# Eighty-eight tiny products on a tile of zeros at the head of TensorE's program

## The chip, the cores and the metric

The kernel runs on one core of a Trainium2 chip. The metric is the device time of one execution in microseconds; before the change its median over 3 runs is 282.65 us (282.52 to 283.0). All stage times below are counted from the first instruction of the one profiled execution.

## What is computed

Eight batches of eight heads of linear attention, and a feed-forward layer on its output:

```python
q_s = softmax of q over its last axis (64)          # q, k, v: (8, 8, 576, 64), float32
k_s = softmax of k over the sequence (576)
kv  = einsum('bhsd,bhse->bhde', k_s, v)
x   = einsum('bhsd,bhde->bhse', q_s, kv)            # as 4608 tokens x 512
h   = x @ w_in                                      # 512 -> 2048
g   = h + sin(alpha * h)**2 / (alpha + 1e-09)
out = g @ w_out                                     # 2048 -> 512
```

## The kernel before

The work is cut in two ways. Attention goes by batch: q, k and v of a batch are loaded as [128, 4, 9, 64] tiles (two heads side by side over the partitions), ScalarE takes the exponentials (`exp_half`, `exp_to`, L117), `kv_mm` (L172) sums k and v over the sequence in 36 small products per half batch, `kv_norm` (L182, L183) divides, and `attn_x` (L216) multiplies the transposed, normalised q (`q_transpose_ii`, L199) by the result. The output goes into `xT`, bf16, with the model dimension on the partitions. The feed-forward part goes by tiles of 512 tokens, nine in all: `mm_h` (L261) makes one of 16 blocks of h from `win` in four accumulating products with the inner index k in the order 0, 2, 1, 3; `sine` (L267, L269 or L271 or L273) and `combine` (L277) make g; `mm_o` (L281) multiplies g by `wout`.

The order on each engine is the order of the program text: nothing is moved by a scheduler. The text is written by hand so that batch 0 is brought through attention first, in halves named `ii`, and then its 512 tokens go through `mm_h` while batch 1 is loaded and worked on.

The head, which the change touches, runs like this:

- SP issues the loads of batch 0 (L306): q half 0, k half 0, q half 1, v half 0, k half 1, then alpha (L311).
- GpSimd builds an identity, VectorE copies it to bf16 (`identb`, L313) and sets `zero` and the ones columns of `vb` (L315, L317). GpSimd then copies one element of the first k half (`held`, L334), which holds it back until that half has landed, and only then issues v half 1 (two DMAs, L306), eight DMAs of `win` (L107: first columns 0 to 511 of k blocks 0 and 2 in two pieces, then of blocks 1 and 3 in one piece of 512 KB, then the rest) and two of `wout` (L110). These convert from float32 to bf16 on the way.
- TensorE starts with seven products of the identity with the first exponentials, 128 weight columns by 512 moving columns each, into a PSUM tile `warm` that nobody reads (`warm_up(7)`, L349). Then come eight transposes of q half 0 (L199), two more such products, `kv_mm` for half 0, one more such product, a small transpose of alpha (L384), eight transposes of q half 1, `attn_x`, `kv_mm` for half 1, the k = 0 and k = 1 products of the first blocks of h, `attn_x` for half 1, and the loop over 16 blocks of h. In the first four blocks the loop adds the last two k.
- In that loop, `late` gives SP the loads of batch 1: q half 0 behind block 6, q half 1 and then k and v in halves (L452) behind block 12, each behind a VectorE write of one element into the buffer (L443).

Behind that loop stands the product with `wout` for the first token tile, interleaved with the attention of batch 1; its two `kv_mm` calls need the casts of v (`cast_v1`, L470, ScalarE and GpSimd), and each cast needs its half of v.

Of the kernel before, what the change touches and what calls it, by code (L numbers as in the profile page):

```python
# [16 lines left out]
BF16 = mybir.dt.bfloat16  # L17
# [6 lines left out]
def kernel(  # L24
# [14 lines left out]
    nc = tc.nc  # L39
# [15 lines left out]
    singles = ctx.enter_context(tc.tile_pool(name="singles", bufs=1))  # L55
# [249 lines left out]
    def load0(eng, n, t, ii, j0=0, j1=J):  # L305
        eng.dma_start(out=staged[n, 0][:, ii::2, j0:j1].rearrange("p i j d -> p i (j d)"),  # L306
                      in_=src_view(t, 0)[:, ii::2, j0 * D:j1 * D])

    for n, t, ii in (("q", q, 0), ("k", k, 0), ("q", q, 1), ("v", v, 0), ("k", k, 1)):
        load0(nc.sync, n, t, ii, 0, 8 if n == "q" else J)  # L310
    nc.sync.dma_start(out=alpha_rows, in_=moe_alpha.rearrange("(no ni) -> no ni", ni=128))  # L311
    make_identity(nc, ident)
    DVE_CP(identb, ident)  # L313
    zero = singles.tile([128, 1], F32, name="zero")
# [8 lines left out]

    tp0 = ps_h[0].tile([128, 8, 128], BF16, name="tp", tag="a")
    warm = ps_h[0].tile([128, 4, 128], F32, name="warm", tag="a")

# [380 lines left out]
```

## Time and profile before

| | us |
|---|---|
| median of 3 runs (range) | 282.65 (282.52 to 283.0) |
| the profiled execution's own time | 282.79 |
| its span, first to last instruction | 281.0 |
| outside the span | 1.8 |
| TensorE busy in the span | 267.7 (95%) |
| ScalarE, VectorE, GpSimd busy | 223.8, 185.5, 81.3 |
| HBM traffic, mean over the span | 164 GB/s |

The profile's busy time of TensorE is an upper view, since matmuls are pipelined and overlap in it: a product of 512 moving columns shows as 379 ns, while in a dense stretch the next one starts 216 ns later (eight of them span 1.73 us in the chain of waits). A line of the timeline gives the start, the length, the engine, the line, the operation with its output and inputs, the count, and in brackets the idle time of the engine ahead of it and what ended that. The views used are the chain that ended last, the timeline, the waits, the busy time by windows and the DMA queues. The trace also holds one record for each DMA packet; the sixteen 4-byte packets with which a load signals its end (one for each DMA engine) show when each of the sixteen engines finished its part.

### The profile page before, as it was taken

What the parts mean: (1) busy time and instruction counts of PE and PEld (TensorE: products, weight loads), DVE (VectorE), ACT (ScalarE), POOL (GpSimd) and SP (SyncE); (2) the same over time, 40 slices, a digit from 0 to 9 for tenths busy, and PEclk for the clock granted to TensorE, in tenths of its full rate; (3) what the DMA queues carried; (4) which work ended last, traced back from release to release, by engine and by line L of the source; (5) the groups of instructions that cost most, each with busy time, mean ns of one, the idle gap of its engine ahead of it and who ended that gap; (6) DMA issues with size and microseconds to landing.
All of it is one profiled execution on the core that took longest, in us unless ns stands there. A gap on an engine that the chain in (4) does not pass through costs nothing.

```text
span 281.0 us, 4925 instructions
## 1 busy us (share of the span) xinstructions
PE 267.7 (95%) x1890; PEld 124.0 (44%) x1919; DVE 185.5 (66%) x279; ACT 223.8 (80%) x322; POOL 81.3 (29%) x77
## 2 busy tenths in 40 slices
PE   2899989999999999999999999999999999999994
PEld 1444444444443444444444444444444444444443
DVE  3968776899878767766776677577775555555412
ACT  5899458999588999899989998999877777777400
POOL 2968121777667460205003500350000000000000
PEclk9999999999999999999999999999999999999999
DMA  7999999997599039712991199125011111111143
GB/s 263 299 194 232 278 307 319 361 343 253 120 229 399 2 81 334 290 37 48 267 383 45 37 263 392 38 50 124 8 29 40 37 37 37 40 41 42 40 106 75
DMA packets 39320, 45.82 MB, mean 163 GB/s; under 512 B 17008, under 2 KB 22656, under 8 KB 39296
## 3 DMA queue, kind: packets, MB, share of 16 engines
q1 hardware_dynamic: 33392, 40.58, 46.9%
q0 software_dynamic: 5744, 4.79, 10.3%
q8 instruction: 15, 0.25, 0.3%
q10 hardware_dynamic: 160, 0.13, 0.2%
q14 instruction: 9, 0.07, 0.1%
HBM read 36.71 MB, written 9.44 MB: 164 GB/s over the span
## 4 chain that ended last, share of the span: by engine, by line
PE 85%; DMA 8%; POOL 2%; issue 1%; SPq 1%; ACT 1%; DVE 1%; ACTq 0%
PE op L281 38%; PE hp L261 38%; DMA st_v<-in_v_dram 4%; DMA win<-in_moe_w_in_dram 2%; PE lp L261 2%; PE kvp L172 2%; DMA st_k<-in_k_dram 2%; PE op L261 1%; PE op L679 1%; POOL s L271 1%; PE kvp L261 1%; PE hp L216 1%; PE xp L216 1%; POOL st_v L306 1%; DVE g L277 1%
## 5 line engine op out<-in xcount | busy, mean ns | idle before, releaser
L277 DVE SCALAR_TENSOR_TENSOR g<-s,inva_sb,hp 128x512 bf16<-128x512 f32 x128 | 94.5, 746 | 58.7 <-ACT s L269 53.3
L261 PE MATMUL hp<-xT,win 128*128 128x512 bf16 x506 | 127.7, 379 | 0.6 <-PE lp L216 0.2
L281 PE MATMUL op<-wout,g 128*128 128x512 bf16 x478 | 121.0, 379 | 1.6 <-issue 1.1
L267 ACT ACTIVATE s<-hp,alpha_sb 128x512 f32<-128x512 f32 x128 | 86.1, 682 | 22.3 <-PE hp L261 21.0
L261 PEld LDWEIGHTS <-win 128*128 128x128 bf16 x576 | 55.7, 98 | 67.8 <-DMA win<-in_moe_w_in_dram 1.2
L281 PEld LDWEIGHTS <-g 128*128 128x128 bf16 x560 | 53.4, 98 | 64.8 <-issue 2.3
L269 ACT ACTIVATE s<-s 128x512 f32<-128x512 f32 x112 | 70.5, 630 | 3.5
L271 POOL TENSOR_TENSOR s<-s 128x512 f32<-128x512 f32 x29 | 30.1, 1053 | 17.6 <-ACT s L267 11.3
L151 POOL TENSOR_TENSOR qn<-qe,qs 128x1152 bf16<-128x1152 bf16 x11 | 23.2, 2127 | 29.5 <-DVE qs L145 24.4
L293 DVE COPY o<-op 128x512 f32<-128x512 f32 (+2 forms) x33 | 21.8, 661 | 10.2 <-PE op L281 7.9
L136 POOL CAST vb<-st_v 128x1152 bf16<-128x1152 f32 x12 | 14.7, 1257 | 45.6 <-DMA st_v<-in_v_dram 45.6
L117 ACT ACTIVATE qe<-st_q 128x1152 bf16<-128x1152 f32 (+2 forms) x18 | 17.7, 1025 | 6.1 <-DMA st_q<-in_q_dram 6.0
L117 ACT ACTIVATE ke<-st_k 128x1152 bf16<-128x1152 f32 x16 | 17.9, 1151 | 3.2 <-DMA st_k<-in_k_dram 3.2
L144 DVE TENSOR_REDUCE qs<-qe 128x36 f32<-128x2304 bf16 x5 | 12.8, 2551 | 8.3 <-ACT qe L117 8.3
L117 ACT ACT_TABLE_LOAD x7 | 9.0, 1283 | 0.8 <-PEq L693 0.7
L172 PE MATMUL kvp<-vb,ke 64*64 64x65 bf16 x576 | 6.9, 194 | 2.2 <-ACT vb L470 1.5
L349 PE MATMUL warm<-qe,identb 128*128 128x512 bf16 x10 | 4.1, 554 | 5.0 <-ACT qe L117 5.0
L281 PE MATMUL hp<-wout,g 128*128 128x512 bf16 x31 | 8.6, 379 | 0.1
L172 PEld LDWEIGHTS <-ke 64*64 64x64 bf16 x576 | 6.0, 106 | 6.1 <-issue 3.4
L281 PE MATMUL lp<-wout,g 128*128 128x512 bf16 x30 | 8.4, 379 | 0.2 <-issue 0.2
L261 PE MATMUL lp<-xT,win 128*128 128x512 bf16 x30 | 7.5, 379 | 0.1
L229 DVE CAST xT<-xp 128x1024 bf16<-128x1024 f32 (+1 forms) x7 | 7.4, 1065 | 0.0
(89 smaller groups left out, 135.8 us busy)
## 6 DMA issues: line engine op xcount, KB each, us to landing
out_dram<-o SPq DMA_DIRECT2D x70, 128.0 KB, 2.4
st_q<-in_q_dram SPq DMA_DIRECT2D x6, 1152.0 KB, 6.3
st_k<-in_k_dram SPq DMA_DIRECT2D x6, 1152.0 KB, 8.6
st_v<-in_v_dram SPq DMA_DIRECT2D x6, 1152.0 KB, 11.3
st_k<-in_k_dram SPq DMA_DIRECT2D x4, 576.0 KB, 8.1
st_q<-in_q_dram SPq DMA_DIRECT2D x4, 512.0 KB, 6.0
st_v<-in_v_dram SPq DMA_DIRECT2D x3, 576.0 KB, 10.0
wout<-in_moe_w_out_dram POOLq DMA_DIRECT2D x3, 512.0 KB, 12.7
```

What stands on the lines that cost most here:

```text
L117: nc.scalar.activation(dst[:, :, ii * 128:(ii + 1) * 128].rearrange("p j (x d) -> p x j d", x=2), src[:, ii::2], AX.Exp)
L136: engs[ii](vv[:, 2 * ii:2 * ii + 2, :, 0:D], staged["v", b][:, ii::2])
L144: nc.vector.tensor_reduce(qs, A["qe", b].rearrange("p j (i d) -> p j i d", i=4), axis=AXL.X, op=ALU.add)
L151: engs[ii % len(engs)].tensor_tensor(qn[:, ii, 0:j1].rearrange("p j (x d) -> p j x d", x=2), qe[:, ii], part.unsqueeze(3).to_broadcast([12 ...
L172: nc.tensor.matmul(kvp[64 * x:64 * x + 64, e, ii * 65:(ii + 1) * 65], ke[r, j, h * 64:(h + 1) * 64], vt[r, j, h * 65:(h + 1) * 65], start= ...
L261: nc.tensor.matmul(hp, win[:, KO[k], ni * 128:(ni + 1) * 128], xT[:, KO[k], t * MF % NX:t * MF % NX + MF], start=(k == 0), stop=(k == 3))
L267: nc.scalar.activation(s, hp, AX.Sin, scale=alpha_sb[:, ni:ni + 1])
L269: nc.scalar.activation(s, s, AX.Square)
L271: nc.gpsimd.tensor_tensor(s, s, s, op=ALU.mult)
L277: nc.vector.scalar_tensor_tensor(G[t][:, ni], in0=s, scalar=inva_sb[:, ni:ni + 1], in1=hp, op0=ALU.mult, op1=ALU.add)
L281: nc.tensor.matmul(acc, G[t][:, ni, j * 128:(j + 1) * 128], wout[:, ni, :], start=(ni == 0), stop=(ni == nN - 1))
L293: eng(o[:, cols], acc)
```

## The change

A bf16 tile of zeros, `tiny`, is made by VectorE ahead of the copy of the identity. At the head of TensorE's program, ahead of the seven products of `warm_up(7)`, stand 88 products of 64 columns of that tile, as weights, with one moving column of it. They take partitions 0 to 63 and 64 to 127 in turn, write the same half of the partitions of `warm`, one column, and nobody reads the result.

```diff
     nc.sync.dma_start(out=alpha_rows, in_=moe_alpha.rearrange("(no ni) -> no ni", ni=128))
+    tiny = singles.tile([128, 64], BF16, name="tiny")
+    nc.vector.memset(tiny, 0.0)
     make_identity(nc, ident)
     DVE_CP(identb, ident)
...
     warm = ps_h[0].tile([128, 4, 128], F32, name="warm", tag="a")
+    for n in range(88):
+        r = slice(64 * (n % 2), 64 * (n % 2) + 64)
+        nc.tensor.matmul(warm[r, 0, 0:1], tiny[r], tiny[r, 0:1], start=True, stop=True)
```

Each product is two instructions, a weight load and a matmul, so TensorE's program grows from 3839 to 4015 rows, 176 more. VectorE has one instruction more. The order of everything else, on every engine and queue, is as before. All line numbers behind L313 grow by 2 and those behind L325 by 5.

## The prediction

> **What bounds the kernel now.** I read the chain that ended last first, from its start, because the change sits at the head. Each line is start, length, engine and line.
>
> ```profile
> 1.26 4.42 DMA st_k<-in_k_dram
> 5.92 1.56 POOL st_v L306 x2
> 7.48 1.43 POOL win L107 x2
> 8.90 5.92 DMA win<-in_moe_w_in_dram
> 14.87 1.90 PE hp L261 x8
> ...
> 29.41 12.43 DMA st_v<-in_v_dram
> 41.86 0.75 ACT vb L470
> ```
>
> The reader is to see that TensorE is not in the chain for the first 14.87 us. It runs from the k load (landed 5.68) through GpSimd's DMA issues to the 512 KB piece of `win` (landed 14.83). From 14.87 the dense TensorE stream carries it; then the second v half of batch 1, issued at 29.41 and landed at 41.84, sets the end of the stretch. Behind that TensorE alone carries it (85% of the chain).
>
> The timeline of the head, by engine, shows what TensorE does meanwhile.
>
> ```profile
> 4.98 3.15 PE L349 MATMUL warm<-qe,identb 128*128 128x512 bf16 x7 [4.98 <-ACT qe L117]
> ...
> 7.84 0.77 PEld L199 LDWEIGHTS <-qn 128*128 128x128 bf16 x8 [0.62 <-DVE qn L364]
> 7.92 0.87 PE L199 MATMUL tp<-identb,qn 128*128 128x128 bf16 x8
> 8.50 1.17 ACT L331 CAST vb<-st_v 128x1152 bf16<-128x1152 f32 x1 [0.33 <-DMA st_v<-in_v_dram]
> ...
> 9.57 1.00 ACT L378 COPY qT<-tp 128x1024 bf16<-128x1024 bf16 x1
> ...
> 9.72 0.48 PE L172 MATMUL kvp<-vb,ke 64*64 64x65 bf16 x36 [0.50 <-ACT vb L331]
> ...
> 10.61 0.62 PE L199 MATMUL tp<-identb,qn 128*128 128x128 bf16 x8
> ...
> 14.87 3.14 PEld L261 LDWEIGHTS <-win 128*128 128x128 bf16 x16 [0.57 <-DMA win<-in_moe_w_in_dram]
> ```
>
> Two things. The eight transposes take 0.87 at 7.92 and 0.62 at 10.61; the seven warm-up products go at 427 ns start to start (5.79, 6.22, 6.64, 7.07 in the weight loads' lines) where the dense stream goes at 216. So TensorE is at half speed until about 8.5 us and at full speed after. (The granted clock reads 1.00 in the windows from 0 on, so the half-speed stretch is seen only in durations.) And every step of this stretch waits for something else: the transposes for VectorE's `qn` (7.80), `kv_mm` for ScalarE's cast (9.66), which waited for v's DMA; the stream at 14.87 for `win`.
>
> **The change, part by part.**
>
> *The memset.* One short VectorE instruction (the two memsets of 36 columns took 0.09 each) ahead of the identity copy, which waits for GpSimd until 1.34 while VectorE is idle. Nothing.
>
> *The 88 products on TensorE.* The trace has no such shape. Below: `kv_mm`'s 36 products of 64 weight columns and 65 moving ones took 0.41 us in the windows view (9.72 to 10.13), 11.4 ns each at full speed with four quarters of the array in turn; 88 of them 1.0 us. Above: the half-speed transposes, 107 ns each (seven steps from 7.92 to about 8.6), 9.4 us. I take the nearer row, `kv_mm`, times two for half speed and two for using two quarters, not four: 46 ns, 4.0 us. Starting near 0.9 (VectorE is free at 0.75) they end near 4.9, when the first exponentials release the warm-up (4.98). TensorE was idle there, so they cost nothing. An end 1 us later is still hidden: warm-ups at full speed take 1.5 us instead of 3.0, and the first hard date is the transposes at 7.84. At the upper bound they would end at 10.3, and the head would slip by some 2.5 us; I give that 3%.
>
> *What an earlier full clock saves.* Warm-ups 1.5 us, transposes 0.4, ending near 8.4 instead of 8.8. Their reader, ScalarE's copy, starts at 9.57 because ScalarE is in the cast until 9.67. So what is late next is the same cast, and the saving on the path is 0. From 8.6 on TensorE is at full speed in both. If the products don't raise the clock, the cost is also 0.
>
> [...]
>
> *176 more instructions to fetch.* This is the part that touches the path. The page's queue list:
>
> ```profile
> q8 instruction: 15, 0.25, 0.3%
> ```
>
> Fifteen packets of 16.4 KB (0.25 MB over 15) against 3809 recorded TensorE instructions on the page: one packet for 254 instructions, so this is TensorE's code. By the trace's packet records they start at 15.93, 37.62, 49.25 and so on and take 0.9 to 1.3 us each on one DMA engine. They are requested ahead of need: by the fourth (67.91) 1042 instructions had already started. I expect no code stall. But each holds up the engine that carries it. By the 4-byte end packets, from the 15.93 packet on one engine finishes each load later than the other fifteen: 20.65 against 19.87, 23.19 against 22.42, and, with the second packet at 37.62, the last v half at 41.45 against 40.03. That late engine is what landed v at 41.84.
>
> With 176 instructions ahead, packets come 176 instructions earlier. The first was asked for at some 244 started instructions; 244 - 176 = 68 lies in `kv_mm` (rows 35 to 107, at 9.72). With the same delay of about 1.06 us (14.87 to 15.93) it starts near 10.8. The 512 KB piece of `win` lies then on that engine. Its end packets lie at 13.68 to 14.52; the late engine loses about 1.1 (20.65 against a typical 19.5). If it was among the first twelve (13.68 to 14.06) it ends at 14.8 to 15.2, and the dense stream starts 0.3 to 0.7 later: **+0.45** there. The second packet moves to instruction 454 - 176 = 278, at about 20 us, and may hold the last piece of `win`, wanted at 23.5, by up to 0.9; together up to about **+1.0** at block 12.
>
> What hides it: `kv_mm` idles 0.22 and 1.24 us (waits view, L172 on vb) for v, which lands by that DMA engine's load, not by TensorE. Before 41.45 that engine carried two code packets; now two as well, if the third comes after its last v packet. The third falls at instruction 524 to 531, in `kv_mm` of batch 1 (39.18 to 39.6, or 0.8 later since its v half is then the one delayed), plus 1.06: 40.4 to 41.5, on the edge. A hit costs one packet: 0.5 to 0.95. The later issue of the loads (27.87 to 29.41, behind the stream) can pass on between 0 and its 0.45; DMA ran at 200 to 290 GB/s until 33 and 400 after, so part is made up; I take 0.2.
>
> [...]
>
> *Sum.* 0 (memset) + 0 (products, under the idle 4.98) + 0 (clock, under the cast) + 0.2 = +0.2 us. The profiled execution's 282.79 (281.0 of span and 1.8 outside) gives 283.0; it stands 0.14 above the median, so from the median 282.65 I say **282.9**.
>
> **The rivals.** 0.2%, 0.57 us, is about what a measurement of this kernel can tell from no change.
>
> 1. *No measurable change*, the forecast: 282.1 to 283.2. For: TensorE is off the chain until 14.87 and idle 1.46 us before 42.65. Against: the landing at 41.84 hangs on one engine. 47%.
> 2. *Slower: the third code packet, or the delayed stream, reaches the v landing.* Place: the load of 29.41 to 41.84. Price: 0.5 to 0.95 for the packet, up to 0.45 for the issue; 0.6 to 1.2 together, 283.3 to 283.9. It decides if the packet starts ahead of that engine's last v packet (41.45). For: my estimate straddles it. Against: a v half that comes late delays the request. 34%. With the 3% of products far too slow (285): 37%.
> 3. *Faster: the second code packet leaves the v load.* It sat at 37.62, inside that load. If the engine makes up the earlier packet before 36 (rates fall to 200 GB/s at 29 to 31) and the third misses, v lands 0.9 earlier and the 1.24 us wait shrinks: 281.8 to 282.0. 16%.
> 4. *The products don't raise the clock* (the trace shows no such product, so it can't tell). Same time as 1 or 2, told by the warm-up products' pace; part of those cases.
>
> **Chances and range.** Same 0.47, slower 0.37, faster 0.16. The likeliest case's own range is 282.1 to 283.2; taking in both prices, 281.9 to 284.0.
>
> **What would show it.** The warm-ups at 4.98 starting 216 ns apart, not 427, and the transposes at 7.8 taking about 0.62: the clock step. Those transposes still waiting for `qn` near 7.8 and `kv_mm` for the cast near 9.7: no gain in the head. The first code packet near 10.8 and `win` landing at 15.1 to 15.5: the fetch step. The wait of `kv_mm` near 42.65 shorter than 1.24 with v landing near 41.8: absorbed; landing near 42.5: rival 2; near 41: rival 3. I am wrong if the products run past 7.8, if TensorE's clock falls again in the idle stretch that faster warm-ups leave before 7.8, or if the gap at 14.87 moves for another reason.

## The result and the profile after

The changed kernel takes 284.84 us (median of 14 runs, 283.83 to 286.83), the kernel before 282.88 in the same rounds (14 runs, 281.88 to 285.4): a ratio of 1.0074, 95% interval 1.0056 to 1.0093, or +2.1 us. The forecast of 282.9 and its range up to 284.0 were too low. The profiled execution took 284.82 us with a span of 283.0; before it was 282.79 and 281.0.

The timeline of the head of the changed kernel (start, length, engine, line, operation, idle time ahead of it):

```profile
0.96 2.50 PE L330 MATMUL warm<-tiny 64*64 64x1 bf16 x88 [0.96 <-DVE tiny L313]
...
5.29 3.15 PE L354 MATMUL warm<-qe,identb 128*128 128x512 bf16 x7 [1.83 <-ACT qe L117]
...
8.23 0.99 PE L199 MATMUL tp<-identb,qn 128*128 128x128 bf16 x8
...
10.23 1.17 ACT L336 CAST vb<-st_v 128x1152 bf16<-128x1152 f32 x1 [1.61 <-DMA st_v<-in_v_dram]
11.30 1.00 ACT L383 COPY qT<-tp 128x1024 bf16<-128x1024 bf16 x1
11.45 0.48 PE L172 MATMUL kvp<-vb,ke 64*64 64x65 bf16 x36 [1.80 <-ACT vb L336]
...
12.34 1.00 PE L199 MATMUL tp<-identb,qn 128*128 128x128 bf16 x8
...
16.27 3.78 PEld L261 LDWEIGHTS <-win 128*128 128x128 bf16 x19 [0.23 <-issue]
```

Three things differ from before. The products end at about 3.4 and don't change the clock: the warm-up products still take 3.15 us, and the first transposes 0.99. ScalarE's cast of v half 0, at 8.50 before, starts at 10.23, behind an idle 1.61 us that a DMA ended; TensorE waits 1.80 for it. And the second set of transposes, 0.62 before, takes 1.00: TensorE is at half speed again. The busy time by windows shows that directly, in the column PEclk (third from the right; the others are length, busy time and count of the five engines, and after the clock the DMA share and GB/s):

```profile
9.00:12.00 3.00, 1.20 (x42) 0.71 (x40) 1.91 (x4) 1.77 (x2) 3.00 (x5) 1.00 1.12 332
12.50:15.50 3.00, 2.82 (x51) 1.77 (x49) 2.31 (x6) 2.00 (x4) 2.57 (x4) 0.50 1.36 200
16.00:19.00 3.00, 3.00 (x17) 1.33 (x18) 0.69 (x1) 2.59 (x5) 0.00 (x0) 1.00 1.45 196
```

The second difference, the late cast, starts where the v load was in flight. The DMA queues of the changed kernel between 6.5 and 7.5 us:

```profile
q1 hardware_dynamic: 187, 0.39, 102.9%
...
q8 instruction: 1, 0.02, 6.5%
```

The first packet of TensorE's code starts at 6.89 us by its record (15.93 before), with 187 instructions started, in the middle of SP's loads. Of the sixteen end packets of v half 0, fifteen come between 7.93 and 8.41; the sixteenth not before 9.40; the load has landed at 10.21, and the cast follows at 10.23. Before, all sixteen came between 7.79 and 8.11, and the load had landed at 8.48.

Instruction by instruction, VectorE and ScalarE run the same sequence in both kernels (VectorE but for the memset), so their delays can be followed. They are +0.3 at the first exponentials (4.61 for 4.30; in e9 below, which has no products in the head, the first q load lands as late), +1.73 at the cast and +2.73 where the dense stream starts. Then the waits for v of batch 1 take back part: +1.0 at ScalarE's second cast of v (42.89), +1.1 on VectorE from 44.3 us on. Then it grows again, on ScalarE to +2.0 at 47 us, and stays there to the end. The late part is a wait of ScalarE for the small load of the last q columns (`q8`). First before, then after, from the timeline of ScalarE:

```profile
45.13 0.74 ACT L117 ACTIVATE qe<-q 128x256 bf16<-128x256 f32 x2
```

```profile
47.13 0.72 ACT L117 ACTIVATE qe<-q 128x256 bf16<-128x256 f32 x2 [0.90 <-DMA q<-in_q_dram]
```

TensorE pays for it at the transposes of q8. The waits of TensorE from 44 us on in the changed kernel hold this one line, which before did not have:

```profile
PE tp L544 <- DVE g L277: 0.9, 1, 0.9
```

The third code packet of the changed kernel starts at 43.04 and ends at 43.99, around the issue of the q8 loads; before, it started at 49.25. But the packet is the smaller part of this wait, as the rows of the q8 loads show. First before, then after:

```profile
L515 SPq DMA_DIRECT2D q<-in_q_dram x2: 368/410/452, 41.0 to 41.5; - x2
DMA to landing us min/median/max: 2.5/2.8/3.0
```

```profile
L520 SPq DMA_DIRECT2D q<-in_q_dram x2: 368/536/705, 43.2 to 43.7; - x2
DMA to landing us min/median/max: 2.3/2.8/3.3
```

SP issues these loads behind VectorE's writes into the q8 tile (L519), and those come at 43.05 and 43.11 in place of 40.85 and 40.91: ahead of the last wait for v, where VectorE is still 2.2 us late. So the second load is issued 2.2 us later and takes 0.3 us longer from issue to landing, while ScalarE comes to it only 1.1 us later (46.23 for 45.13). Before, the load could be used some 0.5 us ahead of need. 2.2 + 0.3 - 1.1 - 0.5 gives the wait of 0.9 us, of which the longer load is about a third.

### The profile page after: what moved, and what is told of

The parts are those of the page before. It is cut to its first block, busy times and chain, and to the rows that moved or that the text cites. A ratio compares the mean times of both kernels' runs of the same rounds, so it can differ in the third digit from the quotient of the medians.

```text
span 283.0 us, 5131 instructions
## 1 busy us (share of the span) xinstructions
PE 273.6 (97%) x2007; PEld 127.2 (45%) x2007; DVE 186.0 (66%) x280; ACT 224.2 (79%) x322; POOL 81.0 (29%) x77
## 4 chain that ended last, share of the span: by engine, by line
PE 80%; DMA 6%; issue 4%; ACT 3%; POOL 3%; DVE 2%; SPq 1%; POOLq 0%; ACTq 0%
PE op L281 38%; PE hp L261 35%; DMA st_v<-in_v_dram 6%; POOL s L271 3%; ACT s L267 2%; DVE g L277 2%; PE kvp L172 2%; PE op L261 1%; PE op L684 1%; PE hp L216 1%; PE xp L216 1%; SPq L306 0%; POOL vb L475 0%; ACT vb L336 0%; ACT L411 0%
## 5 line engine op out<-in xcount | busy, mean ns | idle before, releaser
L281 PE MATMUL op<-wout,g 128*128 128x512 bf16 x496 | 123.7, 379 | 0.0
L277 DVE SCALAR_TENSOR_TENSOR g<-s,inva_sb,lp 128x512 bf16<-128x512 f32 x8 | 5.8, 742 | 0.9 <-POOL s L271 0.9
```

Source lines behind the costliest of these rows:

```text
L277: nc.vector.scalar_tensor_tensor(G[t][:, ni], in0=s, scalar=inva_sb[:, ni:ni + 1], in1=hp, op0=ALU.mult, op1=ALU.add)
L281: nc.tensor.matmul(acc, G[t][:, ni, j * 128:(j + 1) * 128], wout[:, ni, :], start=(ni == 0), stop=(ni == nN - 1))
```

## The experiments

The theory after the result (A): the 176 instructions pull TensorE's code packets forward. The first falls into the load of v half 0, the idle stretch that this makes lets the clock fall, and the third falls into the q8 load. That the q8 loads are also issued late is not among these parts. Against A: the products' own busy time costs (B), or the memset and the shifted tiles (C).

One table for all the runs; times in us in the profiled execution of each. "q8: issued, load" is the issue of the first q8 load and the time from issue to landing of the second. The ratio is to the kernel before, measured with it.

| run | code packets 1, 2, 3 start at | v cast starts | q8: issued, load | wait for q8 | ratio (95%) |
|---|---|---|---|---|---|
| before | 15.93, 37.62, 49.25 | 8.50 | 41.02, 3.0 | 0 | 1 |
| the change | 6.89, 20.75, 43.04 | 10.23 | 43.22, 3.3 | 0.90 | 1.0074 (1.0056 to 1.0093) |
| e1 tile only | 15.79, 37.63, 48.63 | 8.74 | 40.95, 2.8 | 0 | 0.9995 (0.9987 to 1.0004) |
| e2 44 products | 14.21, 28.86, 43.10 | 8.74 | 41.42, 3.4 | 0.94 | 1.0032 (1.0022 to 1.0042) |
| e3 six large | 15.52, 36.81, 49.12 | 8.51 | 41.68, 2.9 | 0 | 1.0002 (0.9993 to 1.0011) |
| e4 88 and fill | 6.88, 19.79, 41.64 | 10.21 | 42.07, 3.1 | 0.89 | 1.0047 (1.0029 to 1.0064) |
| e5 80 late | 15.68, 37.46, 44.07 | 8.86 | 41.05, 3.0 | 0 | 1.0015 (1.0002 to 1.0029) |
| e6 nine large | 15.78, 37.62, 48.62 | 8.63 | 41.06, 2.8 | 0 | 0.9998 (0.9986 to 1.0011) |
| e7 110 products | 6.75, 17.44, 41.35 | 10.12 | 41.96, 2.7 | 0.45 | 1.0068 (1.0033 to 1.0103) |
| e8 34 products | 15.47, 32.59, 43.48 | 8.82 | 41.52, 3.8 | 1.35 | 1.0036 (1.0021 to 1.0051) |
| e9 80, earlier | 15.92, 37.78, 41.47 | 8.98 | 42.09, 3.5 | 1.17 | 1.0041 (1.0028 to 1.0054) |
| e10 32 columns | 5.33, 22.09, 44.50 | 10.19 | 45.16, 3.3 | 1.08 | 1.0138 (1.0115 to 1.0160) |
| e11 88, q8 early | 6.83, 20.80, 45.26 | 10.21 | 36.41, 7.5 | 0 | 1.0251 (1.0221 to 1.0281) |
| e12 the same and fill | 6.98, 20.00, 44.34 | 10.36 | 35.71, 7.6 | 0 | 1.0244 (1.0227 to 1.0262) |
| e13 q8 early, order kept | 6.90, 20.96, 43.68 | 10.28 | 36.67, 7.2 | 0 | 1.0067 (1.0047 to 1.0086) |
| e14 the same and fill | 6.80, 20.04, 42.90 | 10.18 | 35.56, 7.2 | 0 | 1.0039 (1.0020 to 1.0059) |
| e15 before, q8 early | 15.76, 37.39, 48.81 | 8.57 | 33.85, 8.5 | 0 | 1.0029 (1.0004 to 1.0053) |

**e1, the tile without the products.**

```diff
-    for n in range(88):
-        r = slice(64 * (n % 2), 64 * (n % 2) + 64)
-        nc.tensor.matmul(warm[r, 0, 0:1], tiny[r], tiny[r, 0:1], start=True, stop=True)
```

> The tile of zeros and its memset stay, all 88 products go. Theory A (the 176 added instructions pull TensorE's first code packet forward, from 15.9 us to 6.9 us, into the load of v half 0, and the idle stretch that this makes lets the clock fall): no products, no shift of code, so the time of the kernel before within 0.2%, first code packet near 15.9. Theory B (the products themselves, TensorE busy from 0.95 to 3.4 us, hold up the start or the loads): also the time before. Theory C (the memset, or the 128 bytes by which later tiles move in memory): the whole +2 us stays.

282.31 against 282.48: no difference. C falls.

**e2, 44 products.** The range is 44.

> 44 tiny products in place of 88, so 88 instructions more than before. The first code packet was asked for at some 183 started instructions (6.89 us after the change, 187 started). Theory A: 183 - 88 = 95 lies in the first kv product group at 9.7 us, the packet comes at 10 to 12 us, behind v half 0, so the v cast starts near 8.5 to 8.8 as before and kv near 9.8; what is left of the loss is that the packet meets the third piece of w_in: +0.2 to +1.0 us. Theory B: half the products, half the loss, about +1.0 us, with the v cast late by about 0.9. The place of the v cast tells them apart.

The cast starts at 8.74 and `kv_mm` follows at once: nothing is late in the head. So the head's loss is not in proportion to the products. The packet came later than I expected, at 14.21, behind the piece of `win` that the stream starts with; the next piece is then waited for, and the q8 load as well:

```profile
16.76 2.27 PEld L261 LDWEIGHTS <-win 128*128 128x128 bf16 x12 [0.43 <-DMA win<-in_moe_w_in_dram]
```

The +0.9 us that this run loses comes with the q8 wait (0.94; the loads are issued 0.4 later than before and take 0.4 longer) and the same wait of 0.9 at the q8 transposes. That is where the theory got its third part.

**e3, six large products in place of the tiny ones.**

```diff
-    tiny = singles.tile([128, 64], BF16, name="tiny")
-    nc.vector.memset(tiny, 0.0)
+    zeros = singles.tile([128, 512], BF16, name="zeros")
+    nc.vector.memset(zeros, 0.0)
...
-    for n in range(88):
...
+    for n in range(6):
+        nc.tensor.matmul(warm, zeros[:, 0:128], zeros, start=True, stop=True)
```

> 6 products on zeros with 128 weight columns and 512 moving columns in place of the 88 tiny ones: 12 instructions instead of 176, TensorE busy for about as long (6 x 0.427 = 2.6 us against 2.4). Theory A: the first code packet moves by 12 instructions only, stays at 12 to 16 us, the v cast starts near 8.5 and the time is that of before within 0.3% (if the clock opens earlier, the warm-up products go at 216 ns and nothing is gained on the path). Theory B: the loss of +2 us stays, since TensorE is as busy as with the tiny products.

TensorE is busy for 2.7 us in the head, longer than with the 88, and the time is that of before. B falls: TensorE's busy time in the head costs nothing.

**e4, the change with the gap filled.** Nine warm-up products in place of two ahead of the first kv group.

```diff
-    warm_up(2)
+    warm_up(9)
```

> The changed kernel with 9 warm-up products in place of 2 ahead of the first kv group (14 instructions more), which fill the 1.8 us for which TensorE waited for the v cast. Theory A in two parts, code packet and clock: the code packet still lies in the load of v half 0 (near 6.9 us) and the cast is as late (10.2), but the clock doesn't fall at 12.4 us; of the +2.0 us some 0.5 to 0.9 are recovered, so +1.1 to +1.5 against before. If the whole loss comes from the clock: back at the time before. If the clock has no part in it: +2.0 or a little more.

The cast is as late (10.21), the clock stays at 1.00, and the dense stream's delay is +1.7 in place of +2.7 (VectorE's sequence). At the end +1.3 us is left of +2.1 (1.0047 against 1.0074; the intervals overlap). The clock has a part of some 0.8 us.

**e5 and e9, aimed at the third packet.** No products in the head; 80 tiny ones ahead of a kv group of batch 1, in `kv_mm` (e5: `(1, 1)`, e9: `(1, 0)`); the tile is made as in the change.

```diff
+        for n in range(80 if (b, ii) == (1, 0) else 0):
+            r = slice(64 * (n % 2), 64 * (n % 2) + 64)
+            nc.tensor.matmul(kvp[r, n % 2, 300:301], tiny[r], tiny[r, 0:1], start=True, stop=True)
```

> No tiny products in the head; 80 of them right ahead of the second kv product group of batch 1, where TensorE waited 1.24 us for v (80 x 13 to 28 ns = 1.1 to 2.2 us). The first two code packets stay (near 15.9 and 37.6), the third comes forward from 49 us to about 43, into the load of the last q columns (q8, issued at 41.0). Theory A with its second step (the late part of the loss is the third packet in that small load): ScalarE's exponentials of q8 wait 0.8 to 1.0 us for the load, the transposes of q8 wait for VectorE near 57 us, and the time rises by 0.5 to 1.0 us. Rival (what is late there is what the head left over): no shift in the head, so no loss, within 0.2% of before.

> As the run that put 80 tiny products ahead of the second kv group of batch 1, whose third code packet came at 44.07, just behind the q8 load; now they stand ahead of the first kv group of batch 1 (39.2 us), so that the packet comes 1.5 to 2.2 us earlier, 41.9 to 42.6, inside the q8 load. TensorE pays about 1.1 us there, of which the 1.24 us wait for v further on takes back all or nearly all. Theory A, second step: ScalarE waits 0.4 to 1.4 us for q8, the transposes of q8 wait near 57 us, and the time rises by 0.5 to 1.0 us. Rival (the third packet does nothing): no wait for q8, at most the part of the 1.1 us that isn't taken back, 0 to 0.3 us.

e5 missed its aim: the packet came at 44.07, too late to hold the load up (3.0, as before), and there is no wait for q8 (the remaining +0.15% is not explained). e9 hit it. The head and the first two packets are as before, TensorE's extra 1.1 us are gone by 43 us (VectorE's sequence at -0.02), and then ScalarE waits:

```profile
46.13 0.72 ACT L117 ACTIVATE qe<-q 128x256 bf16<-128x256 f32 x2 [1.17 <-DMA q<-in_q_dram]
```

The transposes of q8 wait 1.0 us, and the time is up by 1.2 us (1.0041). So a wait for q8 needs nothing late in the head; VectorE's sequence in e9 is at +0.99 behind this wait, and another 0.45 comes up further on that I did not trace. It isn't the packet alone, though: the 80 products hold up VectorE's write ahead of the q8 loads as well, which go out 1.07 us later (42.09). The load itself is 0.5 us longer than before (3.5 for 3.0), and that is what the packet can have cost here.

**e6, nine large products.** As e3 with `range(9)`, so that TensorE is busy without a break from 1.2 us into the warm-ups.

> 9 large products on zeros instead of the 88 tiny ones (18 instructions), end to end with the warm-up products: TensorE busy without a gap from 1.2 to 8 us. Theory A, and the prediction's step that an earlier clock saves nothing: the clock opens between 5 and 8 us, at least some of the seven warm-ups run at 216 ns, and the time is that of before within 0.2%. If an earlier clock were worth something: faster by 0.4 us or more. If busy TensorE alone costs: slower by over 0.5 us.

This does what the change seems meant to do. The timeline of TensorE:

```profile
5.14 1.67 PE L353 MATMUL warm<-qe,identb 128*128 128x512 bf16 x7
8.01 0.62 PE L199 MATMUL tp<-identb,qn 128*128 128x128 bf16 x8 [1.20 <-DVE qn L368]
8.47 0.59 PE L353 MATMUL warm<-qe,identb 128*128 128x512 bf16 x2
9.85 0.48 PE L172 MATMUL kvp<-vb,ke 64*64 64x65 bf16 x36 [0.79 <-ACT vb L335]
```

By the pace of the products the clock is full from about 5.1: the warm-ups take 1.67 in place of 3.15, the transposes 0.62 in place of 0.87, and all of it goes into longer waits for VectorE (1.20) and ScalarE (0.79). Ratio 0.9998: an earlier clock is worth nothing here.

**e7, 110 products.** The range is 110.

> 110 tiny products, 220 instructions. The 183rd instruction starts near 3.5 us, so the first code packet should come near 4.3 us, inside the loads of k half 0 and q half 1. Theory A: k half 0 lands late on one DMA engine (by about 1 us, 6.7 in place of 5.7), GpSimd is held longer, all of w_in is issued later, v half 0 stays late as well; the time is 1.0 to 2.5 us above before. Theory B (cost goes with the products' own busy time): 110/88 of +2.0, +2.5 us, without a late k load. The landing of k half 0 tells them apart.

The time is within what both theories gave, but the place was wrong: the packet came at 6.75 and not at 4.3, k half 0 landed as before (`held` starts at 5.89, before 5.73), and v half 0 is late as with 88. So the count of instructions started when the packet begins doesn't carry over from run to run, as I had taken it to; the last section has a count that fits better.

**e8, 34 products.** The range is 34.

> 34 tiny products, 68 instructions: chosen so that the first code packet stays clear of v half 0 (12 to 14.5 us), the second leaves the loads of batch 1 (near 31 in place of 37.6) and the third comes behind the q8 load (near 45; the q8 load is complete by about 44). Theory A: nothing late in the head, v half 1 of batch 1 lands up to 0.7 earlier, no wait for q8: between -0.6 and 0 us against before. Theory B (products cost by themselves): +0.8 us, below the 44 products' +0.9 in proportion.

The first two packets fell as planned, the third at 43.48 in place of 45, into the q8 load, and the wait of 1.35 came with it: +1.0 us. As a version to beat both kernels it failed, and the number is nearer to theory B's +0.8, which e3 and e10 rule out by other means. For the third part it is the clearest run: the q8 loads are issued 0.5 us later than before and the second takes 3.8 in place of 3.0, the longest of the runs that issue them there, with the packet inside it.

**e10, the same 176 instructions with half the work.**

```diff
-        nc.tensor.matmul(warm[r, 0, 0:1], tiny[r], tiny[r, 0:1], start=True, stop=True)
+        nc.tensor.matmul(warm[64 * (n % 2):64 * (n % 2) + 32, 0, 0:1], tiny[r, 0:32], tiny[r, 0:1], start=True, stop=True)
```

> The changed kernel with 32 weight columns in each of the 88 products in place of 64: the same 176 instructions, about half of TensorE's work in them (1.2 us in place of 2.4, if a product's time goes with its columns). Theory A (code packet, then clock): first packet between 5.5 and 7 us, v cast late by 1.2 to 1.8, time +1.6 to +2.4 us as with 64 columns. Theory B (what counts is the products' own time): about half, +1.0 us, and the v cast late by half.

The products took 1.33 us in place of 2.50, the packet came earlier still (5.33), into q half 1, and the loss grew to +3.9 us. In this run the clock stayed low for two stretches, as two windows show:

```profile
12.50:15.50 3.00, 2.29 (x49) 1.80 (x50) 1.70 (x4) 1.71 (x3) 2.73 (x4) 0.50 1.35 197
16.00:19.00 3.00, 3.00 (x11) 0.87 (x10) 0.87 (x3) 1.36 (x3) 0.00 (x0) 0.50 1.45 196
```

Half the work and nearly twice the loss: B is out. Where the extra loss comes from is only in part seen. The packet lies in q half 1 here, whose exponentials come 1.2 us later than in the change; TensorE waits 0.98 for the load of alpha, which it did not there; and the clock is low for two steps and not one.

**e11 and e12, the q8 loads earlier.** The issue is moved up behind the first normalisation of q of batch 1; e12 has the fill of e4 too.

```diff
         q1_norm(0)
+        for b in range(2):
+            DVE_CP(q8[:, 0, b, 0:1], zero)
+            nc.sync.dma_start(out=q8[:, :, b], in_=src_view(q, b)[:, :, 8 * D:J * D])
         q1_sums(1)
```

> The changed kernel with the q8 loads issued earlier (behind the first normalisation of q of batch 1, some 37 to 39 us, in place of 43), so that the third code packet near 43 can't hold them up. Theory A (three parts: first packet in v half 0, clock, third packet in the q8 load): head as late as before (cast 10.2, clock low from 12.4 us in most executions), but no wait for q8; of the +2.0 us some 0.7 to 1.0 goes, +1.0 to +1.4 is left. Rival (the late loss isn't the q8 load): +2.0 stays.

> The same with 9 warm-up products in place of 2 ahead of the first kv group as well, so that the clock doesn't fall. What is left of theory A's parts is the late v half 0 alone, which the later waits for v of batch 1 should take back in large part: 0 to +0.6 us against before. If parts are missing from theory A: +0.8 or more.

Both failed as experiments. In the program text the loads of batch 2 stand right behind those of q8 on SP, so they also went out 5.2 to 7.8 us earlier than in the change, while a piece of `wout` had not landed yet; the waits of TensorE in e11 name it:

```profile
PE hp L281 <- DMA wout<-in_moe_w_out_dram: 3.7, 1, 3.7
```

**e13, e14 and e15, the same with the loads of batch 2 held where they were**, and a control without the products.

```diff
-        load_batch(2)
+        load("q", q, 2, gate=DVE_CP)
+        load("k", k, 2)
+        load("v", v, 2)
```

> The changed kernel with the q8 loads issued earlier, and the loads of batch 2 held at their old place by a VectorE write into the q buffer (in the run before, moving q8 let them go out 6 us earlier, ahead of the last piece of w_out, for which TensorE then waited 3.7 us). Theory A: no wait for w_out and none for q8; of the changed kernel's +2.0 us some 0.6 to 1.0 goes, +1.0 to +1.4 left. Rival (the q8 load has no part in the loss): +2.0 stays.

> The same with 9 warm-up products in place of 2 ahead of the first kv group. Theory A: the late v half 0 alone is left, and the later waits take back most of it: -0.2 to +0.6 us against before. If the head's delay reached the end by itself: +1.0 or more.

> The control: the kernel before, without the 88 products, with the same two moves of loads. Theory A: the third code packet (49 us) doesn't touch the q8 load here, so that moving it gains nothing: within 0.2% of before. If the moves by themselves are worth 0.6 us or more, the two runs beside it say nothing of the code packet.

The control is not neutral: 1.0029 (0.8 us), with a wait of 0.9 us for `wout`. By what was set down for it, a control that far off makes e13 and e14 say nothing of the code packet; and e13's own +1.9 us is what the rival gave. What can be done is to read them against the control and not against before. Over the control, the change without the q8 wait costs 0.38% (1.1 us), and without q8 wait and fallen clock 0.10% (0.3 us). Each of these differences carries the uncertainty of two intervals of some 0.2% each, so the division is rough: of +2.1 us, about 1.0 goes with the wait for q8, about 0.8 with the clock, and about 0.3 is what the later waits leave of the late v half 0. The profile of the change agrees on the first: TensorE is 0.99 us late ahead of the q8 transposes and 2.00 behind them. e4 gives the second as 0.8 by another way.

Moving the q8 loads takes away both causes of that wait, the late issue and the third packet, so these runs don't divide the 1.0. The load times in the table do, roughly: without a third packet near it the second q8 load takes 2.8 to 3.0, in the change 3.3, in the others with a wait for q8 2.7 (e7) to 3.8 (e8). So the third packet's own share in the change can be put at some 0.3 to 0.5 us; it is not shown by itself, since no run puts the third packet into that load without delaying its issue too. The rest of the 1.0 is the head's delay again, passed on by VectorE's write; e4 has nearly the whole wait (0.89) with a load of 3.1, issued 1.05 us late.

## Why the prediction was wrong

- **What bounds the kernel** held: TensorE is not on the path in the head, and loads are (e3 1.0002, e6 0.9998).
- **The memset** costs nothing (e1, 0.9995), as said.
- **The products** take 28 ns each (2.42 us from the first weight load to the last, over 88), not 46; hidden all the same. The two factors of two in the 46 were estimates; no run shows by itself what using two quarters in place of four does. That they would not raise the clock was rival 4, and it is what happened: 3.15 us for the warm-ups.
- **An earlier clock saves 0**: right, and shown by e6, which got the clock (1.67 us for the warm-ups) and not a gain (0.9998).
- **The code packets** were the right mechanism at the wrong place, and this is the step that failed: the place of the first packet, and with it the +0.2 us that was the whole sum. I took the 244 instructions started when the packet *began* as the point at which it is *asked for*, added 1.06 us, and got 10.8 us and the piece of `win`. It began at 6.89, in the load of v half 0, and the time went up by 2.1 us. In the change the packet started with 187 instructions begun, in e7 with 233, in e10 with 181, 2.7 to 3.4 us after the tiny products ended (3.5, 4.0 and 2.3 us). So the count at the packet's start differs from run to run and tells little, and no run shows that a packet starts 1.06 us after it is asked for. With that open, the bound should have reached back to the end of the products. That would have put v half 0, which `kv_mm` waits for with 0.50 us of idle already, among the loads at risk.
- **The size** for one engine (1.1 us) was somewhat too small: v half 0 landed 4.1 to 4.3 us behind k half 0 in the eight runs whose packet lies ahead of 7 us, against 2.7 to 2.9 in the nine others; that is 1.2 to 1.6 us. The casts came at 10.1 to 10.4 against 8.5 to 9.0.
- **The fallen clock** stood in the last sentence as a way to be wrong, without a price. It fell not in the gap ahead of 7.8, which I named, but behind the gap of 1.80 us that the late v made (0.50 from 12.42 to 15.83); about 0.8 us.
- **What hides it** was right for the waits for v: +2.7 at the stream start is down to +1.1 behind them. It left out the q8 loads, which I had not priced at all: two DMAs of 128 KB, 2.8 us to landing, with ScalarE and then its table load of 1.28 us behind them. VectorE's write releases them ahead of the last of those waits, 2.2 us late, and so they carry the head's delay past the place where it was to be absorbed. I looked for the third packet in the load of v half 1 only; it came at 43.04, and the second q8 load was 0.3 to 0.5 us longer than in the runs without a packet near it. Together that is about 1.0 us.
- **Rival 2** had the sign, but its place was the landing of v of batch 1, and that is not where the time was lost. Its price of 0.6 to 1.2 us left out the clock and the q8 loads.

No version here beats both kernels; e1, e3 and e6 tie with the one before.

## What to carry to other kernels

The 88 products ended 1.83 us ahead of the next product's release here, and their 176 instructions still moved its first code packet from 15.93 to 6.89 us. The packet, 16.4 KB and 1.05 us, fell into the load of v half 0, which ended by 8.41 on fifteen DMA engines and not before 9.40 on the sixteenth. In a stage that waits for loads, count instructions as well as microseconds: six large products kept TensorE busy here for as long as the 88 small ones (2.74 us against 2.50), at no cost (1.0002). When a short gap opens on TensorE, price the clock that may fall behind it along with the gap: here one of 1.80 us was followed by 3.41 us at a clock of 0.50, and about 0.8 us was lost with that. And when a later wait is to take back a delay, look for loads that are issued ahead of that wait: here the q8 loads went out 2.2 us late, and about 1.0 us was lost with them, the third packet's share included.

## What the runs showed of the hardware

- The clock record changes at steps of 3.413 us: in the change it stands at 0.50 from 12.42 to 15.83 us, one step, and at 1.00 for 78 of them (266.24 us) behind it. Over such a step, TensorE busy for 1.62 us of 3.42 (the change, 9.00 to 12.42), 1.47 (e10) and 1.35 (e13) was followed by a step at half speed, as was 0.89 (e12) and 1.18 and 0.81 (e11); 2.02 (e11), 2.21 (e6, 5.08 to 8.49), 2.52 (e6) and 2.81 (before, 8.45 to 11.87) was not. The step of the change that lost the clock, then one of e11 that kept it and one that lost it (TensorE's busy time is the second number):

```profile
9.00:12.42 3.42, 1.62 (x45) 0.93 (x44) 2.29 (x5) 2.19 (x3) 3.31 (x5) 1.00 1.16 318
42.13:45.54 3.41, 2.02 (x51) 1.06 (x48) 1.95 (x5) 1.84 (x3) 0.62 (x1) 1.00 1.11 324
45.54:48.95 3.41, 0.81 (x4) 0.29 (x3) 0.18 (x1) 0.00 (x0) 0.00 (x0) 1.00 1.06 374
```

So in these rows the clock was lost behind steps that were busy for 0.81 to 1.62 us, though TensorE was not idle in them, and kept behind steps with 2.02 to 2.81; no step here lies between. At half speed 2.42 us in a step (e10) didn't bring the clock back. And 1.58 us of busy time in the step from 2.18 to 5.59 of the changed kernel, tiny products and warm-ups, didn't open it.

- Which executions lose the clock varies. Of the change's 14 runs, eight show a mean clock of 0.988 to 0.994, at 284.77 to 286.83 us; of the six at 1.00, four lie at 283.83 to 284.43 and two at 285.62 and 285.92, which the clock doesn't explain.
- In the change the first code packet took 1.05 us by its record; in the eight runs that have it ahead of 7 us, v half 0 landed 1.2 to 1.6 us later than in the others, and in the change it was one DMA engine of sixteen that ended late. Why by more than the packet's own time stays open.
- When the first packet is asked for shows in no trace; an estimate can be made from its start. In sixteen of the seventeen runs it starts 3.2 to 4.1 us after the start of TensorE's 178th recorded instruction (4.1 before, 3.6 in the change; 5.0 in e8); counts down to about 140 fit nearly as well, those above 180 don't. So, as an estimate, a request at a fixed count with a delay of 3 to 4 us fits, in place of the 244 and 1.06 us of the prediction. For the second packet the same count plus 254 (one packet for 254 instructions, as the prediction has it) gives 1.4 us before and 1.2 in the change, so the delay isn't fixed, and no run here separates the request from the start.
